# A new order of phase 1 in a linear-attention and SwiGLU block

## The chip, the cores and the metric

One core of a Trainium2 chip runs the whole kernel. The metric is the device time of one execution in microseconds (us), as a median over runs. One execution was also profiled, and its rows are what the argument below uses.

## The reference

A block on x of 2048 rows and 512 columns in bf16: a layer norm, a linear attention of 32 heads of 16 columns, and a SwiGLU feed-forward with 1792 hidden columns, both added to x.

```python
xn = layernorm(x)                                  # no gain, eps 1e-5
q, k, v = split(xn @ wqkv)                         # 32 heads of 16
phi = lambda t: where(t > 0, t + 1, exp(t)) + 1e-6
kv  = einsum("bhsd,bhse->bhde", phi(k), v);  z = phi(k).sum(over s)
o   = (phi(q) @ kv) / (phi(q) . z + 1e-6)
out = x + o @ wo + (silu(xn @ w_gate) * (xn @ w_up)) @ w_down
```

## The kernel before

The rows are cut into 16 tiles of 128. In phase 1 each tile t is normalised, turned so that its columns lie on the partitions, and projected to q and k; phi is applied; and G = xn^T phi(k) is summed over all tiles in four PSUM banks (0 to 3). v is never formed: G times the v weights gives kv afterwards. Phase 2 loops over 56 steps j (four chunks of 512 rows by 14 slices of the hidden columns): gate and up matmuls (`gu`, L526), SiLU on ScalarE (L534), the product on VectorE (`hop`, L539), and between them the output tiles (`ogroup`, L656 and L660).

Every operation goes through `K.add`, which records it with the tiles that it reads and writes. Each engine then runs its own operations strictly in the order of recording, and waits on semaphores where an operation needs another engine's result. So the order of phase 1 is one string of steps, written out by hand, that is read from left to right. Each word is a letter and a tile number, and goes to one engine:

- `S` (VectorE: row statistics, L251 and L254), `R` (ScalarE: rstd, L262 and L264), `L` (VectorE, L320) or `P` (GpSimd: a small step L335 and the normalising L338): xn of a tile.
- `D` (SyncE queue, L401): a DMA transpose of xn into `xnT`, by which tiles 4 to 15 get ready for their projections and tiles 0 to 2 for phase 2.
- `K`, `Q` (TensorE, L423): the projection of a tile to k or q, four matmuls of 512 columns into one bank; `K0:2` is only its part of weight chunk 2. The banks 4 to 7 are used in turn, so a projection also waits until the phi sum of the fourth before it has read its bank.
- `x`, `m`, `s` (for k) and `y`, `n`, `u` (for q): phi as exp on ScalarE (L441 or L444), a minimum on GpSimd (L451), and the sum on VectorE (L462).
- `G` (TensorE, L472): a tile's four matmuls into G.
- `l`, `T` (SyncE queue): loads of a tile of x, and of the large weights: T0 and T4 the halves of the gate weights, T1 and T5 those of the up weights, T2 the v weights, T3 wo, T6 the down weights.
- `U` (TensorE, ScalarE, VectorE): a step j of phase 2 done early.
- `F` (TensorE, L241): matmuls on constants that keep the engine busy; seven of them also open the kernel.

Tiles 0 to 2 (CENTRED) start the kernel, ahead of their statistics. Their x is only centred; the scale is applied later in phi. Tiles 0 and 2 are turned on TensorE by matmuls with the identity (`c`, L376), to which `d` (L384) adds minus the mean, taken from `nmb`, one column that either `M` (ScalarE, a copy of the tile with a running sum, L367), `O` (GpSimd, L370) or `a` (VectorE, L370) has written. Tile 1 has its mean from `M1` (ScalarE, L277), is centred by `C1` (VectorE, L292) and turned by `W1` (TensorE, L350). `e` and `h` (ScalarE, L393) take the two halves of tiles 0 and 2 out of PSUM into `xcT`, and `w`, `v`, `Y`, `Z` do it for whole tiles; tile 3 goes by `X3` and `Y3`. `j` (VectorE) and `J` (GpSimd, L312 and L315) make the centred and scaled tiles that G needs.

The first loads go out from two queues: four tiles of x and the eight 128 KB chunks of the q and k weights (`Q0` to `Q3`, `K0` to `K3`), six on SyncE's and six on ScalarE's.

Of the kernel before, what the change touches and what calls it, by code (L numbers as in the profile page):

```python
# [111 lines left out]
def bass_parallel_sum__linear_attn_block__swiglu_ffn__prompt_kernel(nc, A_x, A_wqkv, A_wo, B_x, B_w_gate, B_w_up, B_w_down, out):  # L112
# [5 lines left out]
    with contextlib.ExitStack() as es:  # L118
# [67 lines left out]
        def xload(eng, t):  # L186
            load(eng, ("x", t), x_sb[:, t, :], xin[t * P:(t + 1) * P, :])
# [22 lines left out]
        def wchunk(eng, i, c):  # L210
            load(eng, ("wqk", i, c), wqkv[:, c, i * D:(i + 1) * D], A_wqkv[c * P:(c + 1) * P, i * D:(i + 1) * D])

        for eng, text in (("sp", "x0 x1 Q0 Q3 K3 K0"),
                          ("act", "x2 Q1 x3 Q2 K2 K1")):
            for w in text.split():
                if w[0] == "x":
                    xload(eng, int(w[1:]))
                else:
                    wchunk(eng, int(w[0] == "K"), int(w[1:]))
# [336 lines left out]
        def run(text):  # L556
            words = [(w[0], int(w[1:].split(":")[0]), [int(c) for c in w.split(":")[1]] if ":" in w else None)
                     for w in text.split()]
            late = {t for k, t, _ in words if k == "z"}
            later.update({t: i for i, t in enumerate(t for k, t, _ in words if k == "u" and t in late)})  # L560
            for k, t, cs in words:
                steps[k](t) if cs is None else steps[k](t, cs)

        run("""
            M1 l4 c2 S0 c0 O0 S2 d0 a2 e0 d2 Q0:1 l13 e2 h0 Q0:0 C1 S1 l5 h2 W1 l7 Q2:01 Q0:3 S3 Q0:2 l11 R0
            Q2:3 Q2:2 r0 K0:2 l14 R3 j2 j0 K0:3 y0 J1 w1 L3 n0 K2:23 S4 y2 K0:01 l9 K2:1 K2:0 x0 x2 n2 X3 Y3
            K1:3 S13 m0 u0 Q1:123 m2 K1:12 K1:0 l6 R13 P13 s0 x1 s2 u2 T1 R4 Q1:0 l8 m1 K3 S9 y1 s1 l10 R9 x3 S5
            Q3 P4 D13 L9 D4 n1 G0 m3 y3 G2 G1 n3 u1 s3 P1 K13 Q13 x13 m13 K4 u3 G3 y13 S7 R5 s13 S14 D9 P5 K9 Q4
            S10 x4 m4 s4 n13 x9 u13 T2 G13 G4 D5 R10 K5 l12 R7 m9 P10 l15 y4 R14 Q9 P14 s9 Q5 S8 S6 x5 n4 D10 G9
            m5 u4 Q10 y9 R6 S15 y5 P7 s5 G5 R8 L6 y10 n9 u9 S12 K10 P0 n5 x10 n10 D14 u5 m10 D7 L8 D6 u10 D8 s10  # L570
            K14 Q14 K7 x14 T0 R15 D0 m14 y14 s14 Q6 S11 n14 x7 y6 u14 G14 R12 R11 m7 K8 P11 n6 s7 K6 Q7 L15 x6
            G7 x8 m6 D15 u6 s6 m8 Q8 D11 L2 P12 y8 n8 s8 y7 G6 K15 x15 n7 K11 m15 D12 x11 G10 u8 u7 m11 K12 T3
            Q11 s15 G8 y11 s11 x12 Q15 y15 Q12 m12 s12 D1 n11 D2 u11 n15 G11 G12 u15 y12 n12 T6 u12 T5 U0 U1 G15
            T4
        """)

        def gt_evac(c, eng):
# [181 lines left out]
```

## Time and profile before

| what | value |
|---|---|
| median of 3 runs | 212.54 us (212.4 to 212.63) |
| profiled execution, its own time | 212.36 us |
| its span in the profile | 211.1 us |
| TensorE busy | 206.5 us, 98% |
| VectorE, ScalarE, GpSimd busy | 122.3, 66.2, 67.4 us |

The execution's own time is 1.26 us more than its span, which runs from the first instruction to the last. In the rows below PE is TensorE's matmuls, PEld its weight loads, DVE VectorE, ACT ScalarE, POOL GpSimd, and SPq the issue of a DMA by SyncE. A row of the timeline is: start in us, duration in us, engine, line, operation, out<-in, shapes, count, and in brackets the idle time before it and what ended that. A row of the waits is: who waited for whom, us in total, times, the longest. A row of the DMA view is: tensors, queue and kind, count, KB of each, and the median us from issue to landing.

### The profile page before, as it was taken

How to read it: one execution, taken by the hardware profiler on the slowest of the kernel's cores; microseconds unless marked ns; L12 is line 12 of the kernel's file. 1: busy time of each engine (PE TensorE's matmuls, PEld its weight loads, DVE VectorE, ACT ScalarE, POOL GpSimd, SP SyncE). 2: the span in 40 equal slices, each digit the busy share in tenths (PEclk: the TensorE clock that was granted, in tenths of full speed). 3: DMA queues.
4: the chain of work that ended last, by engine and by line, in shares of the span. 5: the costliest groups of instructions: out<-in, count | busy, mean ns of one | idle time of the engine just before them, and what ended most of it. 6: DMA issues, size and time to landing. Idle time of an engine off the chain costs nothing.

```text
span 211.1 us, 2710 instructions
## 1 busy us (share of the span) xinstructions
PE 206.5 (98%) x992; PEld 96.2 (46%) x1011; DVE 122.3 (58%) x223; ACT 66.2 (31%) x135; POOL 67.4 (32%) x94
## 2 busy tenths in 40 slices
PE   7999999999999999999999999999999999999996
PEld 3444344444544444444444444444444444444455
DVE  3999986654885368454644773464457463625122
ACT  3985656454354333031221322130123031220000
POOL 3597776749950162202202021202202210000000
PEclk9999999999999999999999999999999999999999
DMA  6965739399501201110101110111001111011101
GB/s 183 361 203 151 126 66 233 64 285 366 184 0 25 53 0 27 22 50 28 25 25 42 32 30 25 25 48 26 28 26 24 25 50 51 3 50 26 49 28 50
DMA packets 28733, 16.43 MB, mean 78 GB/s; under 512 B 18608, under 2 KB 28592, under 8 KB 28720
## 3 DMA queue, kind: packets, MB, share of 16 engines
q1 hardware_dynamic: 27856, 15.48, 27.3%
q10 hardware_dynamic: 864, 0.79, 1.2%
q8 instruction: 8, 0.13, 0.3%
q14 instruction: 5, 0.04, 0.1%
HBM read 9.96 MB, written 2.10 MB: 57 GB/s over the span
## 4 chain that ended last, share of the span: by engine, by line
PE 93%; DMA 3%; ACT 1%; issue 1%; POOL 0%; SPq 0%; DVE 0%; POOLq 0%
PE pb L526 46%; PE pb L660 23%; PE pb L423 12%; PE pb L656 7%; PE pb L472 5%; DMA x_sb<-in_A_x_dram 2%; DMA xnT<-xn 2%; PE pb L584 0%; PE pb L650 0%; POOL xn L338 0%; ACT hT L277 0%; ACT ef L444 0%; PE pb L350 0%; SPq L184 0%; DVE out_sb L666 0%
## 5 line engine op out<-in xcount | busy, mean ns | idle before, releaser
L534 ACT ACTIVATE sil<-pb 128x512 bf16<-128x512 f32 x56 | 33.5, 597 | 102.9 <-PE pb L526 101.4
L539 DVE TENSOR_TENSOR hT<-pb,sil 128x512 bf16<-128x512 f32 x56 | 38.2, 683 | 38.9 <-PE pb L526 37.5
L526 PE MATMUL pb<-xnT,wg 128*128 128x512 bf16 x224 | 57.8, 379 | 0.0
L526 PE MATMUL pb<-xnT,wu 128*128 128x512 bf16 x215 | 57.3, 379 | 0.5
L617 POOL TENSOR_TENSOR pz<-pq,zbc 128x512 f32<-128x512 bf16 x16 | 22.3, 1397 | 91.0 <-DVE den L624 79.3
L660 PE MATMUL pb<-wd,hT 128*128 128x512 bf16 (+2 forms) x247 | 51.1, 355 | 0.3
L660 PEld LDWEIGHTS pb<-wd,hT 128*128 128x128 bf16 x252 | 23.6, 98 | 24.9
L526 PEld LDWEIGHTS pb<-xnT,wu 128*128 128x128 bf16 x224 | 21.9, 98 | 26.0
L526 PEld LDWEIGHTS pb<-xnT,wg 128*128 128x128 bf16 x224 | 21.9, 98 | 25.8
L666 DVE TENSOR_TENSOR out_sb<-pb,x_sb 128x512 bf16<-128x512 f32 (+2 forms) x18 | 11.4, 632 | 35.8 <-PE pb L660 35.8
L423 PE MATMUL pb<-wqkv,xnT 128*128 128x512 bf16 x103 | 24.0, 379 | 0.4 <-DMA xnT<-xn 0.4
L444 ACT ACTIVATE ef<-pb 128x512 bf16<-128x512 f32 x26 | 15.0, 593 | 13.7 <-PE pb L423 13.7
L451 POOL TENSOR_SCALAR ef<-ef 128x512 bf16<-128x512 bf16 x26 | 15.8, 616 | 6.5 <-ACT ef L444 6.5
L656 PE MATMUL pb<-M,pk 128*128 128x512 bf16 (+2 forms) x71 | 16.6, 355 | 0.1
L423 PEld LDWEIGHTS pb<-wqkv,xnT 128*128 128x128 bf16 x104 | 10.0, 98 | 13.1 <-DMA xnT<-xn 0.9
L472 PE MATMUL pb<-pk,xn 128*128 128x512 bf16 x50 | 12.9, 379 | 0.1
L251 DVE BATCH_NORM_STATS2 stats<-x_sb 128x6 f32<-128x512 bf16 x16 | 10.8, 677 | 3.3 <-DMA x_sb<-in_A_x_dram 3.3
L639 DVE TENSOR_TENSOR pq<-pq,rden 128x512 bf16<-128x512 bf16 x16 | 12.6, 786 | 0.0
L462 DVE SCALAR_TENSOR_TENSOR pk<-pb,ef 128x512 bf16<-128x512 f32 x13 | 8.8, 679 | 3.5 <-POOL ef L451 3.5
L462 DVE SCALAR_TENSOR_TENSOR pq<-pb,ef 128x512 bf16<-128x512 f32 x13 | 8.8, 684 | 3.6 <-POOL ef L451 3.5
L624 DVE TENSOR_REDUCE den<-pz 128x32 f32<-128x512 f32 x16 | 10.8, 676 | 0.0
L495 POOL TENSOR_TENSOR zacc<-zacc,pk 128x512 f32<-128x512 f32 x8 | 10.6, 1319 | 0.6
(71 smaller groups left out, 105.4 us busy)
## 6 DMA issues: line engine op xcount, KB each, us to landing
out_dram<-out_sb SPq DMA_DIRECT2D x15, 128.0 KB, 1.7
x_sb<-in_A_x_dram SPq DMA_DIRECT2D x14, 128.0 KB, 4.2
wu<-in_B_w_up_dram SPq DMA_DIRECT2D x2, 896.0 KB, 9.4
wg<-in_B_w_gate_dram SPq DMA_DIRECT2D x2, 896.0 KB, 9.3
wd<-in_B_w_down_dram SPq DMA_DIRECT2D x1, 1792.0 KB, 9.0
wqkv<-in_A_wqkv_dram ACTq DMA_DIRECT2D x4, 128.0 KB, 4.5
wqkv<-in_A_wqkv_dram SPq DMA_DIRECT2D x4, 128.0 KB, 4.2
wqkv<-in_A_wqkv_dram SPq DMA_DIRECT2D x1, 512.0 KB, 4.1
```

The costliest lines, as they stand in the source:

```text
L423: fns.append(lambda e, c=c, first=first, last=last: e.matmul(banks[b][:, :], src[:, c, t * P:(t + 1) * P], wqkv[:, c, col:col + D], start= ...
L444: K.add("act", lambda e: e.activation(buf, banks[b][:, :], ACT.Exp), r=[B(b)], w=[bkey])
L451: K.add("pool", lambda e: e.tensor_scalar(out=buf, in0=buf, scalar1=top, scalar2=0.0, op0=ALU.min, op1=ALU.max), r=[bkey] + tkeys, w=[bkey])
L462: K.add("dve", lambda e: e.scalar_tensor_tensor(out=dst, in0=val, scalar=low, in1=mid, op0=ALU.max, op1=ALU.add), r=keys + lkeys, w=[dkey])
L472: K.add("pe", [(lambda e, c=c: e.matmul(banks[c][:, :], src[:, t, c * P:(c + 1) * P], pk[:, t, :], start=first, stop=last)) for c in range ...
L526: fns.append(lambda e, c=c, b=b, w_=w_: e.matmul(banks[b][:, :], w_[:, c, fc * P:(fc + 1) * P], xnT[:, c, C * 512:(C + 1) * 512], start=(c ...
L534: K.add("act", lambda e: e.activation(sil[:, j % 2, :], banks[gb(j)][:, :], ACT.Silu), r=[B(gb(j))], w=[("sil", j % 2)])
L539: K.add("dve", lambda e: e.tensor_tensor(out=hT[:, C % 2, fc, :], in0=banks[gb(j) + 1][:, :], in1=sil[:, j % 2, :], op=ALU.mult), r=[B(gb( ...
L617: K.add("pool", lambda e: e.tensor_tensor(out=pz[:, t % 2, :].rearrange("q (g p) -> q g p", g=NG), in0=pq[:, t, :].rearrange("q (g p) -> q ...
L639: K.add("dve", lambda e: e.tensor_tensor(out=heads(pq[:, t, :]), in0=heads(pq[:, t, :]), in1=rden[:, i, :][:, :, None].broadcast_to([P, NH ...
L656: fns = [(lambda e, g=g: e.matmul(banks[bank][:, 0:hi - lo], pk[:, t, g * P:(g + 1) * P], M[:, g, lo:hi], start=(g == 0), stop=False)) for ...
L660: fns = [(lambda e, fc=fc: e.matmul(banks[bank][:, 0:hi - lo], hT[:, C % 2, fc, jj * P:(jj + 1) * P], wd[:, fc, lo:hi], start=False, stop= ...
```

## The change

The string of phase 1 is written anew, and the chunks of the weights are dealt anew to the two queues. What is computed stays the same, but for one more constant matmul (`F1`, 256 columns). In the order in which the engines meet it:

- Loads: Q0 and Q1 change queues, and K0, K1 and K3 change places.
- Start: the mean of tile 2 comes from ScalarE (`M2`) instead of VectorE (`a2`). ScalarE runs M2, M1, e0, h0, e2, h2 instead of M1, e0, e2, h0, h2. TensorE starts with Q0:0, F1, Q0:1, Q2:01 instead of Q0:1, Q0:0, W1, Q2:01.
- `J0` (GpSimd) and `j1` (VectorE) take the place of `J1` and `j0`.
- TensorE then runs K13 Q13 K4 K9 G3 Q4 G13 G4 Q9 K5 G9 Q10 Q5 G5 K10 K14 Q14 K7 G10 Q7 K6 G14 Q8 K8 K15 K11 Q6 Q15 Q11 K12 G7 G6 Q12 G8 G12 U0 G11 G15 U1, instead of K13 Q13 K4 G3 K9 Q4 G13 G4 K5 Q9 and so on to U0 U1 G15.
- SyncE's queue runs D13 D4 D9 l15 l12 D5 D10 T2 D14 D7 D6 D8 T3 D15 D1 D11 D0 D12 T0 D2 T6 T4 T5, instead of D13 D4 D9 T2 D5 l12 l15 D10 D14 D7 D6 D8 T0 D0 D15 D11 D12 T3 D1 D2 T6 T5 T4.
- Tiles 7, 11 and 12 are normalised on VectorE and tiles 2 and 6 on GpSimd, where it was the other way round.

```diff
-        for eng, text in (("sp", "x0 x1 Q0 Q3 K3 K0"),
-                          ("act", "x2 Q1 x3 Q2 K2 K1")):
+        for eng, text in (("sp", "x0 x1 Q1 Q3 K1 K3"),
+                          ("act", "x2 Q0 x3 Q2 K2 K0")):
...
         run("""
-            M1 l4 c2 S0 c0 O0 S2 d0 a2 e0 d2 Q0:1 l13 e2 h0 Q0:0 C1 S1 l5 h2 W1 l7 Q2:01 Q0:3 S3 Q0:2 l11 R0
-            Q2:3 Q2:2 r0 K0:2 l14 R3 j2 j0 K0:3 y0 J1 w1 L3 n0 K2:23 S4 y2 K0:01 l9 K2:1 K2:0 x0 x2 n2 X3 Y3
-            K1:3 S13 m0 u0 Q1:123 m2 K1:12 K1:0 l6 R13 P13 s0 x1 s2 u2 T1 R4 Q1:0 l8 m1 K3 S9 y1 s1 l10 R9 x3 S5
-            Q3 P4 D13 L9 D4 n1 G0 m3 y3 G2 G1 n3 u1 s3 P1 K13 Q13 x13 m13 K4 u3 G3 y13 S7 R5 s13 S14 D9 P5 K9 Q4
-            S10 x4 m4 s4 n13 x9 u13 T2 G13 G4 D5 R10 K5 l12 R7 m9 P10 l15 y4 R14 Q9 P14 s9 Q5 S8 S6 x5 n4 D10 G9
-            m5 u4 Q10 y9 R6 S15 y5 P7 s5 G5 R8 L6 y10 n9 u9 S12 K10 P0 n5 x10 n10 D14 u5 m10 D7 L8 D6 u10 D8 s10
-            K14 Q14 K7 x14 T0 R15 D0 m14 y14 s14 Q6 S11 n14 x7 y6 u14 G14 R12 R11 m7 K8 P11 n6 s7 K6 Q7 L15 x6
-            G7 x8 m6 D15 u6 s6 m8 Q8 D11 L2 P12 y8 n8 s8 y7 G6 K15 x15 n7 K11 m15 D12 x11 G10 u8 u7 m11 K12 T3
-            Q11 s15 G8 y11 s11 x12 Q15 y15 Q12 m12 s12 D1 n11 D2 u11 n15 G11 G12 u15 y12 n12 T6 u12 T5 U0 U1 G15
-            T4
+            c2 c0 M2 S0 S2 O0 d0 M1 e0 S1 h0 d2 Q0:0 e2 h2 F1 C1 Q0:1 Q2:01 l4 W1 S3 R0 l13 Q0:3 r0 l6 R3 l10
+            Q0:2 Q2:2 j2 j1 K0:1 y0 l11 L3 K0:2 Q2:3 y2 J0 n0 K2:12 n2 l7 K0:3 K0:0 w1 S4 K2:0 K2:3 K1:013 X3 x0
+            l8 S13 u0 x2 m0 Y3 s0 R13 m2 K1:2 Q1 P13 K3:02 l9 u2 x1 m1 K3:13 s2 S9 R4 l5 Q3 T1 y1 s1 R9 l14 L9
+            D13 x3 P4 D4 n1 G0 S10 G2 m3 y3 D9 n3 G1 K13 u1 s3 u3 x13 l15 S5 P1 m13 s13 Q13 K4 y13 R10 K9 R5 n13
+            G3 Q4 S14 x4 x9 P5 S7 m4 s4 G13 R7 y4 P10 u13 m9 l12 R14 n4 D5 S8 G4 D10 T2 Q9 s9 P2 S6 K5 x5 u4 S15
+            P14 L7 m5 y9 D14 G9 n9 Q10 Q5 R6 s5 u9 y10 S12 D7 R8 G5 K10 y5 n10 u10 L8 P6 K14 n5 x10 m10 x14 D6
+            u5 Q14 y14 D8 R15 s10 K7 S11 G10 L15 R12 x7 m14 s14 Q7 n14 R11 T3 u14 D15 y7 K6 m7 G14 s7 D1 Q8 P0
+            L11 D11 n7 L12 x6 u7 K8 y8 x8 m6 n8 K15 m8 s6 D0 D12 x15 u8 K11 x11 s8 m15 Q6 m11 T0 y6 n6 s15 Q15
+            Q11 s11 y15 K12 y11 u6 x12 G7 m12 G6 n11 Q12 y12 G8 s12 D2 T6 n12 n15 G12 u12 U0 G11 G15 u15 u11
+            U1 T4 T5
         """)
```

## The prediction

> **What bounds the kernel now.** First the page: the span, the engines' busy time, the granted clock, and the chain that ended last.
>
> ```profile
> span 211.1 us, 2710 instructions
> PE 206.5 (98%) x992; PEld 96.2 (46%) x1011; DVE 122.3 (58%) x223; ACT 66.2 (31%) x135; POOL 67.4 (32%) x94
> PEclk9999999999999999999999999999999999999999
> PE 93%; DMA 3%; ACT 1%; issue 1%; POOL 0%; SPq 0%; DVE 0%; POOLq 0%
> ```
>
> TensorE is busy for 98% of the span, at the full clock. The change keeps its matmuls (it adds one small one), so it can only win where PE waits. Second, the waits of PE alone:
>
> ```profile
> PE pb L423 <- DMA xnT<-xn: 0.4, 1, 0.4
> PE pb L384 <- DVE nmb L370: 0.3, 1, 0.3
> PE pb L423 <- ACT hT L393: 0.3, 1, 0.3
> ```
>
> That is all, apart from the launch. The whole purse is about 1 us, and each wait has to be found in the timeline. A matmul there lasts longer than its place in the stream, so I take the spacing from a long run: twenty in a row give (4.48 - 0.38) / 19 = 0.216 us each, and a group of four is 0.863 us.
>
> ```profile
> 28.57 4.48 PE L423 MATMUL pb<-wqkv,xnT 128*128 128x512 bf16 x20
> 20.91 1.61 PEld L472 LDWEIGHTS pb<-pk,xn 128*128 128x128 bf16 x8
> 21.13 1.89 PE L472 MATMUL pb<-pk,xn 128*128 128x512 bf16 x7
> 23.39 2.76 PE L423 MATMUL pb<-wqkv,xnT 128*128 128x512 bf16 x12 [0.37 <-DMA xnT<-xn]
> ```
>
> Eight weight loads stand at 20.91 and only seven matmuls at 21.13, so one record is missing. The stream was free again at 21.13 + 8 x 0.216 = 22.86 us, and the next matmul, K5, starts at 23.39. The wait cost 0.53 us, not the 0.37 printed. Third, the chain in order of time says what K5 waited for:
>
> ```profile
> 17.88 0.60 ACT ef L444
> ...
> 19.07 0.76 POOL xn L338
> 19.86 3.48 DMA xnT<-xn
> ```
>
> The transpose of tile 5 (step D5) took 3.48 us. The three before it took 2.4, and the median of all fifteen is 2.5 (first two rows below). In the stretch from 20.8 to 21.9 us a packet of another queue runs among D5's packets: one packet of q8, 5.6% of 16 engines over 1.1 us, which is 0.99 us of one DMA engine.
>
> ```profile
> xnT<-xn SPq DMA_TRANSPOSE x15, 2.5
> xnT<-xn SPq DMA_TRANSPOSE x3, 2.4
> q8 instruction: 1, 0.02, 5.6%
> xnT<-xn SPq DMA_TRANSPOSE x1, 3.5
> ```
>
> That is 3.48 - 2.4 = 1.08 us of delay beside a fetch of 0.99 us: I read it as the share of D5 on that engine standing behind the fetch.
>
> **The change part by part.** *The start.* The first projection starts at 5.89 and waits for L393, which on ACT follows the mean of tile 1 (L277), which waits for x1 to land.
>
> ```profile
> 1.27 3.56 DMA x_sb<-in_A_x_dram
> 4.85 0.63 ACT L277 ACTIVATE hT<-x_sb 128x512 bf16<-128x512 bf16 x1 [2.76 <-DMA x_sb<-in_A_x_dram]
> 5.47 1.19 ACT L393 ACTIVATE hT<-pb 128x256 bf16<-128x256 f32 x4
> 5.89 0.60 PE L423 MATMUL pb<-wqkv,hT 128*128 128x512 bf16 x2 [0.29 <-ACT hT L393]
> ```
>
> The new M2 (0.63 on ACT, plus about 0.19 for its sum) runs in the 2.76 us in which ACT is idle before 4.85, so it costs nothing, and d2 no longer waits for DVE. But M1, e0 and x1 keep their places and slots. PE therefore reaches the same wait earlier and leaves it at the same 5.89: the 0.3 of L384 does not vanish, it merges into the wait for e0. Gain 0. x1, the weights and x2 have equal sizes, 128 KB, and stand in equal slots, so which chunk lands in a slot changes only together with the projection that reads it (Q0:0 and Q0:1 change places). F1 is one matmul of 256 columns, half of the 512 that take 0.216: an estimate of 0.11. It fills time in which Q2:01 would wait for e2, now third on ACT instead of second: e2 ends one L393 pitch, (1.19 - 0.38) / 3 = 0.27, later. F1 costs 0 to 0.11. Against it stands a small stall before K3, the first projection at 11.63:
>
> ```profile
> 9.75 1.45 PEld L423 LDWEIGHTS pb<-wqkv,hT 128*128 128x128 bf16 x8
> 9.80 1.89 PE L423 MATMUL pb<-wqkv,hT 128*128 128x512 bf16 x7
> 11.63 1.89 PE L423 MATMUL pb<-wqkv,xnT 128*128 128x512 bf16 x8
> ```
>
> Eight matmuls from 9.80 end at 11.53, so K3 is 0.10 late for its evacuated tile. Pushed back by F1 it meets that tile in time. Net 0, bounds -0.1 to +0.15.
>
> *The wait at K5.* Before K5 the new order has K13, Q13, K4, K9, G3, Q4, G13, G4, Q9. From the end of Q13 to K5 that is 7 groups, 7 x 0.863 = 6.04 us (before: 6). D5 needs xn5 from POOL: Q13's last matmul drains about 0.2, then y13 0.60 (the L444 row above), n13 0.62, then P5's two steps, whose pitch is 0.30 + 0.76:
>
> ```profile
> 15.95 2.75 PE L423 MATMUL pb<-wqkv,xnT 128*128 128x512 bf16 x12
> 16.37 0.19 POOL L335 TENSOR_SCALAR nm<-mv 128x1 f32<-128x1 f32 x1
> 16.67 0.76 POOL L338 TENSOR_SCALAR xn<-x_sb,nm,rstd 128x512 bf16<-128x512 bf16 x1
> L451 POOL TENSOR_SCALAR ef<-ef 128x512 bf16<-128x512 bf16 x26 | 15.8, 616 | 6.5 <-ACT ef L444 6.5
> ```
>
> Together about 2.5 us after Q13. With a free 2.4 the transpose lands at 4.9 and K5 has 1.1 us to spare. With the whole 3.48 it lands at 5.98 against 6.04, and K5 just makes it or loses 0.1 (its weight load must come first). PE reaches the same count of instructions at about the same time, so the fetch stays where it is, while D5 is issued some 0.3 later (Q13, the second group of the run at 15.95, ended at 15.95 + 8 x 0.216 = 17.7, which makes 20.2 instead of 19.86), so less of the delay remains. I take 0 left of the 0.53; upper bound 0.1.
>
> *The rest of the transposes.* The early x loads change order within a run of equal 128 KB slots, and T1, not needed before U0, goes out one slot later. x15 and x12 leave SP ahead of D5, and T2 (512 KB) now stands behind D10. T3 (wo) comes before D15, D1, D11, D0 and D12, T0 (gate half) after them; T6, T4 and T5 still follow D2. The tightest is D11: xn15 waits for the phi sum of K10 and for S11. From K10's end: 0.2 + x10 0.60 + m10 0.62 + s10 0.68 + S11 0.68 and 0.18 + L15 0.40 = 3.36; D15 and D1 take SP 2.50; D11 needs the median 2.5: 8.36 us. PE has 10 groups between K10 and K11, 8.63 us. Margin 0.3, less 0.1 for the weight load: 0.2.
>
> ```profile
> L462 DVE SCALAR_TENSOR_TENSOR pk<-pb,ef 128x512 bf16<-128x512 f32 x13 | 8.8, 679 | 3.5 <-POOL ef L451 3.5
> L251 DVE BATCH_NORM_STATS2 stats<-x_sb 128x6 f32<-128x512 bf16 x16 | 10.8, 677 | 3.3 <-DMA x_sb<-in_A_x_dram 3.3
> 18.43 0.18 DVE L254 BATCH_NORM_AGGREGATE mv<-stats 128x2 f32<-128x6 f32 x1
> 37.62 0.40 DVE L320 TENSOR_SCALAR xn<-x_sb,mv,rstd 128x512 bf16<-128x512 bf16 x1
> 40.55 2.50 SPq L401 DMA_TRANSPOSE xnT<-xn  x2
> ```
>
> T0 goes out three SP slots after D11 (3 x 1.25 = 3.7) and D2 follows it by 0.6. D0, right behind T0, took 5.6 (first row below; the second is that of the two behind wo), so D2 lands 9.9 after D11's issue; U0 comes 10 groups after K11, at 2.5 + 0.3 + 8.6 = 11.4. It has 1.5 us.
>
> ```profile
> xnT<-xn SPq DMA_TRANSPOSE x1, 5.6
> xnT<-xn SPq DMA_TRANSPOSE x2, 3.9
> 47.57 1.03 PE L526 MATMUL pb<-xnT,wg 128*128 128x512 bf16 x4
> 49.57 0.69 DVE L539 TENSOR_TENSOR hT<-pb,sil 128x512 bf16<-128x512 f32 x1 [1.51 <-PE pb L526]
> ```
>
> U1 needs the bank of Q15, freed by u15, which on DVE now follows the product of U0. That product starts 2.00 after U0 (49.57 - 47.57) and u15 ends 0.6 + 0.69 later, at 3.3; U1 comes after U0, G11 and G15, at 4 x 0.863 = 3.45. Margin 0.15, less the weight load. DVE loses an operation on one column and gains one normalising of 0.40, POOL loses one, ACT gains M2: all of it lies under PE, as DVE is busy for 58% of the span.
>
> *Sum.* 212.36 (the profiled execution: span 211.1 and 1.26 around it) - 0.53 + 0 + 0 = 211.83 us. The median of the runs shown, 212.54, stands 0.18 above that execution, so I forecast 212.0 as a median, 0.25% faster. A measurement of this kernel can tell about 0.2% from no change, 0.42 us: the forecast lies only just beyond it.
>
> **A rule against it.** The Trainium skill, "Runtime: NRT & Kernel Launch", section "Instruction fetch mechanics", says that each engine is refilled in blocks of 256 instructions ahead of use, and that the cost of crossing a block is mostly hidden. By it the fetch would not be what made K5 wait, and the first rival below is left; the rows above (0.99 of fetch, 1.08 of delay) speak for the fetch.
>
> **The rivals.** *The load did it.* T2 went out on SP 2.66 us ahead of D5.
>
> ```profile
> 17.20 0.58 SPq L184 DMA_DIRECT2D wqkv<-in_A_wqkv_dram  x1
> wqkv<-in_A_wqkv_dram SPq DMA_DIRECT2D x1, 512.0 KB, 4.1
> ```
>
> If T2 delayed D5, the delay moves with it to D14, now the next transpose behind it. D5 landed 23.34 - 17.20 = 6.1 us after T2's issue; T2 now leaves one slot, 1.25, after D10, so D14 would land 7.4 after D10's issue. D10 leaves about 4.2 after Q13's end (D5's 2.5, then m4 0.62 and P10 1.06), and K14 comes 13 groups, 11.2, after it: 7.0. K14 waits 0.4 instead of K5's 0.53: 212.23, as a median 212.4. Against it: T2 had landed by 17.20 + 4.1 = 21.3, when a free D5 would still have had 1.0 us to go.
>
> *Small new waits.* K11, U1 and K3 have margins of 0.1 to 0.2 us, and my sums are no better than that. Each could lose 0.1 to 0.2: 0.1 to 0.4 in all, medians of 212.1 to 212.4.
>
> *Slower: wo ahead of D11.* The two transposes behind wo took 3.9 in the median (row above) against 2.5. If D11, third behind it, takes that too, K11 is late by 3.9 - 2.5 - 0.2 = 1.2, and 212.36 - 0.53 + 1.2 = 213.03, as a median 213.2. It turns the result beyond 0.2% once D11 takes more than 2.5 + 0.2 + 0.53 + 0.42 = 3.65. For it: 0.2 us of margin. Against it: D11 is issued at least 3.1 us after wo (its own 0.58 and two slots), and a load of that size lands in about 4.1.
>
> **How the numbers follow.** Forecast 0.58, the load 0.07, small new waits 0.20, wo ahead of D11 0.15. The forecast case is faster, and so is the first 0.02 of the small waits: 0.60. The rest of them and the load fall within 0.2%: 0.25. Slower 0.15. The range starts at 211.7 (the start's bound of -0.1, and 0.2 of spread between executions) and ends at 212.9, where the case of wo begins to turn the sign: left out are the worse part of that case and about 0.05 below.
>
> **What would show it.** In the profile after: no wait of PE on DMA xnT; the first projection still at about 5.9 us behind L393, with L384 no longer waiting; a D5 of 2.4 to 3.5 us with K5 right behind Q9; U0 near 46.2 us (47.57, less G11, less 0.53, give or take 0.1). A wait of PE on a DMA transpose at K14 speaks for the load, one at K11 for wo, and one on DVE L462 at U1 for the small waits. I am wrong if PE's waits after 6 us come to more than 0.1.

## The result and the profile after

The changed kernel takes 211.97 us (median of 9 runs, 211.54 to 212.37), the kernel before 212.54 in the runs beside it (9 runs, 212.34 to 213.18). The ratio is 0.9969, with a 95% interval of 0.9956 to 0.9981: faster by 0.3%. The profiled execution of the changed kernel took 211.76 us, against 212.36.

First the page of the changed kernel (span, busy time, the chain that ended last), then all that PE itself waited for:

```profile
span 210.5 us, 2725 instructions
PE 207.9 (99%) x1012; PEld 96.7 (46%) x1012; DVE 124.4 (59%) x223; ACT 67.2 (32%) x137; POOL 66.0 (31%) x92
...
PE 99%; DVE 0%; issue 0%
...
PE pb L241 <- PEq L744: 0.8, 1, 0.8
```

The chain, which was 93% PE with 3% DMA, is now PE from end to end, and the only wait left is the launch. (F1 is the one new matmul. The page counts 20 more because 19 matmul records are missing in the profile of the kernel before, which has 992 beside 1011 weight loads; the changed kernel's has 1012 of each.) The timeline of PE around the two places where time could change:

```profile
5.57 0.61 PE L423 MATMUL pb<-wqkv,hT 128*128 128x512 bf16 x1
5.97 0.35 PE L241 MATMUL pb<-const-bfloat16-1.0 128*128 128x256 bf16 x1
6.16 0.81 PE L423 MATMUL pb<-wqkv,hT 128*128 128x512 bf16 x3
...
11.57 1.89 PE L423 MATMUL pb<-wqkv,xnT 128*128 128x512 bf16 x8
...
21.07 1.89 PE L472 MATMUL pb<-pk,xn 128*128 128x512 bf16 x8
22.79 1.89 PE L423 MATMUL pb<-wqkv,xnT 128*128 128x512 bf16 x8
24.52 1.03 PE L472 MATMUL pb<-pk,xn 128*128 128x512 bf16 x4
...
46.10 1.03 PE L526 MATMUL pb<-xnT,wg 128*128 128x512 bf16 x4
```

K3 (11.57) starts 0.06 earlier than before (11.63). The eight matmuls from 21.07 end at 21.07 + 8 x 0.216 = 22.80 and Q9 and K5 follow without a gap: the 0.53 us is gone. 0.53 + 0.06 is the whole difference of the spans, 0.6.

The DMA view around the first stretch shows what became of D5 and of the fetch on queue q8. The fetch is the one large packet: 16 KB, in the slice marked 328 (slices of 0.05 us from 19.0, so at 19.6), after the last packets of x12.

```profile
GB/s 369 369 389 328 246 226 164 103 41 0 0 0 328 0 0 0 0 0 0 0 0 164 0 0 0 0 0 0 0 0 0 0 0 0 0 0 0 0 0 0
...
q8 instruction: 1, 0.02, 4.1%
...
xnT<-xn SPq DMA_TRANSPOSE x1, 2.4
```

It ran from 19.63 to 20.95 and was over before D5's packets began at 21.40; D5 was issued at 20.22 and landed at 22.65, in 2.4 us instead of 3.5. The rate of the DMA over the same three microseconds, 20.2 to 23.2 in slices of 0.075 us, first of the kernel before, then of the changed one:

```profile
GB/s 410 369 341 273 219 150 82 82 246 0 0 55 160 218 191 222 184 232 181 130 55 11 7 10 7 10 10 10 119 7 10 17 11 0 0 123 232 232 232 273
```

```profile
GB/s 0 0 0 0 0 0 0 0 0 0 0 0 0 0 0 3 92 198 232 225 212 218 218 198 109 39 4 0 0 0 0 0 0 0 0 0 0 72 188 225
```

This is what a held-up transpose looks like. Both show D5 as a hump of about 0.7 us near 200 GB/s. In the kernel before the hump has a tail: from 21.8 us, which is where the fetch (20.85 to 21.84) ends, the rate stands at 7 to 17 GB/s for 0.8 us (the 119 in it is one 8 KB packet of another queue, q14). The records of the single packets say what the tail is: D5 moves in 512 packets of 256 bytes, and exactly 32 of them, one sixteenth, begin after the fetch's end, one behind the other until 22.65. I read that as one DMA engine out of 16 doing its share alone, after the fetch. The transpose lands, at 23.34, only when that share is done. The hump itself is not late: D5's packets begin 1.2 us after its issue in both kernels (21.05 and 21.40), with T2 ahead of it or not.

### The profile page after: what moved, and what is told of

It reads as the page before. It is cut to its first block, busy times and chain, and to the rows that moved or that the text cites. A ratio compares the mean times of both kernels' runs of the same rounds, so it can differ in the third digit from the quotient of the medians.

```text
span 210.5 us, 2725 instructions
## 1 busy us (share of the span) xinstructions
PE 207.9 (99%) x1012; PEld 96.7 (46%) x1012; DVE 124.4 (59%) x223; ACT 67.2 (32%) x137; POOL 66.0 (31%) x92
## 4 chain that ended last, share of the span: by engine, by line
PE 99%; DVE 0%; issue 0%
PE pb L526 46%; PE pb L660 23%; PE pb L423 13%; PE pb L656 7%; PE pb L472 7%; PE pb L241 2%; PE pb L384 0%; PE pb L584 0%; PE pb L650 0%; PE pb L376 0%; PE pb L350 0%; DVE out_sb L666 0%
## 5 line engine op out<-in xcount | busy, mean ns | idle before, releaser
L251 DVE BATCH_NORM_STATS2 stats<-x_sb 128x6 f32<-128x512 bf16 x16 | 10.9, 678 | 3.5 <-DMA x_sb<-in_A_x_dram 3.4
```

## The experiments

Each was timed in five rounds beside the kernel before, whose median there was 212.54 to 212.66. "Span from K3" in the table is the span of the profiled execution less the start of K3, the first projection from `xnT`: it takes the start out, which varies between 11.24 and 11.99 us. The fetch is the start of the first 16 KB packet on q8, D5 its time from issue to landing.

| kernel | K3 | span from K3 | fetch | D5 | loss behind K3 | ratio and interval |
|---|---|---|---|---|---|---|
| before | 11.63 | 199.5 | 20.85 | 3.48 | K5 0.53 | |
| after | 11.57 | 198.9 | 19.63 | 2.44 | none | 0.9969 (0.9956 to 0.9981) |
| e1 | 11.39 | 199.0 | 18.80 | 2.42 | none | 0.9962 (0.9948 to 0.9977) |
| e2 | 11.72 | 199.5 | 20.93 | 3.46 | K5 0.51 | 0.9987 (0.9970 to 1.0003) |
| e3 | 11.50 | 199.6 | 19.14 | 2.42 | K13 0.62 | 0.9976 (0.9950 to 1.0002) |
| e4 | 11.61 | 199.0 | 19.37 | 2.42 | none | 0.9955 (0.9939 to 0.9971) |
| e5 | 11.53 | 199.0 | 20.78 | 3.36 | none | 0.9972 (0.9959 to 0.9986) |
| e6 | 11.70 | 199.5 | 19.84 | 2.44 | Q13 0.57 | 0.9990 (0.9977 to 1.0002) |
| e7 | 11.99 | 199.5 | 21.16 | 3.47 | K5 0.52 | 1.0003 (0.9988 to 1.0017) |
| e8 | 11.79 | 199.1 | 19.79 | 2.43 | 0.14 at 13.5 | 0.9974 (0.9962 to 0.9987) |
| e9 | 11.98 | 199.4 | 19.91 | 2.43 | last output 0.43 | 0.9994 (0.9983 to 1.0005) |
| e10 | 11.97 | 199.2 | 20.86 | 3.21 | K5 0.26 | 0.9997 (0.9982 to 1.0013) |
| e11 | 11.42 | 199.0 | 19.28 | 3.26 | none | 0.9976 (0.9965 to 0.9986) |
| e12 | 11.24 | 199.4 | 19.70 | 2.58 | last output 0.43 | 0.9991 (0.9974 to 1.0008) |

198.95 plus the loss in its row gives each "span from K3" within 0.1, so nothing else behind K3 moved the span by more than that. All of a row but its ratio comes from one profiled execution.

Theory A is the prediction's: the fetch runs at its own time and holds up D5; K5's later place saves the 0.53. Theory B is the first rival: the load T2, going out ahead of D5, does it. What the first runs led to is theory C: T2 holds the fetch back until it runs into D5, so both are needed, and either moving T2 or moving K5 is a cure.

**e1: only T2 is moved**, in the kernel before.

```diff
-S10 x4 m4 s4 n13 x9 u13 T2 G13 G4 D5 R10 K5 l12 R7 m9 P10 l15 y4 R14 Q9 P14 s9 Q5 S8 S6 x5 n4 D10 G9
+S10 x4 m4 s4 n13 x9 u13 G13 G4 D5 R10 K5 l12 R7 m9 P10 l15 y4 R14 Q9 P14 s9 Q5 S8 S6 x5 n4 D10 T2 G9
```

> The kernel before with one step moved: T2 (the v weights, 512 KB) goes out behind D10 instead of ahead of D5, as in the changed kernel. Fetch theory (D5 stands behind TensorE's first instruction fetch on one DMA engine): D5 still takes 3.3 to 3.5 us, K5 still waits about 0.5, 212.5 us, ratio 1.000. Load theory (D5 stands behind T2): D5 takes 2.4 to 2.5, K5 does not wait, 212.0, ratio 0.9975.

It took 211.9 us. PE's waits, then the DMA view from 18.0 to 19.6 (slices of 0.04 us):

```profile
PE pb L241 <- PEq L744: 0.8, 1, 0.8
```

```profile
GB/s 0 0 0 0 0 0 0 0 0 0 0 0 0 0 0 0 0 0 0 410 0 0 0 0 0 0 0 0 0 0 0 0 0 0 0 0 0 0 0 0
...
q8 instruction: 1, 0.02, 3.8%
```

With no load about, the fetch is alone in the stretch, at 18.8, and is over before D5's packets. One step moved in one string brings a gain that the runs can't tell from the whole change's. T2 had a part in it, against theory A.

**e2: fourteen more instructions ahead of the fetch**, in the kernel before: the seven filling matmuls as fourteen of half the width.

```diff
-        keep_busy(NWARM, 512)
+        keep_busy(2 * NWARM, 256)
```

> The kernel before with the seven opening matmuls of 512 constant columns cut into fourteen of 256: the same columns, seven more pairs of instructions ahead of the work. Fetch theory: the first fetch of q8 comes 7 x 0.216 = 1.5 us earlier in the work, at about 19.3, and is over before D5's packets start at about 21.0; D5 takes 2.4 to 2.5, K5 does not wait, 212.0 us, ratio 0.9975. Load theory: D5 still takes 3.5, 212.5 us, ratio 1.000.

212.47 us. Only TensorE has more instructions here, and the later fetches of q8 came earlier, the third by 1.6 us (67.87 instead of 69.51), the others by 0.1 to 7.9: q8 brings TensorE's instructions. The first fetch did not move: 20.93, and T2 landed at 21.37. K5 waited as before:

```profile
PE pb L423 <- DMA xnT<-xn: 0.3, 1, 0.3
```

So, with T2 ahead of it, the count of instructions doesn't set the first fetch's place.

**e3: the changed kernel with 23 narrow filling matmuls**, to put the fetch on D9.

```diff
-        keep_busy(NWARM, 512)
+        keep_busy(23, 156)
```

> The changed kernel with the opening 3584 constant columns cut into 23 matmuls of 156: 16 more pairs. Fetch theory: the first fetch comes 16 x 0.216 = 3.5 us earlier, at about 16.2 to 17.5, among D9's packets; D9 takes 3.3 to 3.5 instead of 2.5 and lands at about 19.1, K9 (due at 18.5) waits 0.4 to 0.6, and the time goes back to 212.4 to 212.6, ratio to before 1.000. Load theory: nothing changes, D9 takes 2.5, 212.0, ratio 0.9975.

A miss: the fetch moved by half a microsecond, to 19.14, and D9 took 2.51. In the profiled execution D13 took 3.75 us with no fetch on record beside it, and K13 waited:

```profile
16.43 1.90 PE L423 MATMUL pb<-wqkv,xnT 128*128 128x512 bf16 x8 [0.46 <-DMA xnT<-xn]
```

The load that left SP last before it landed 1.3 us later there than in the changed kernel (15.77 instead of 14.45), and D13 landed 0.62 behind that load. The median, 211.97, is the changed kernel's, so that execution was not a usual one. Why the load was late stays open.

The added instructions did put a later fetch on a transpose where no load is about, in phase 2. The transpose issued at 91.89 took 3.18 us; its counterpart in the changed kernel, with no fetch beside it, took 2.42. The DMA view of e3 from 91.9 to 95.0 us (slices of 0.0775 us; the lone 211 is the fetch, 92.33 to 93.54) has the same hump and tail as D5's:

```profile
GB/s 0 0 0 0 0 211 0 0 0 0 0 0 0 0 0 66 198 208 221 221 225 221 165 56 26 0 13 20 10 10 10 20 0 0 0 1 1 0 0 0
...
q8 instruction: 1, 0.02, 2.4%
...
pk<-pq SPq DMA_TRANSPOSE x1, 3.2
```

All loads have landed by 60 us. Of the 238 transposes behind that in the fourteen traces, 18 have a 16 KB fetch running between 1.0 and 2.4 us after their issue, and took 2.54 to 4.19 us; the other 220 took 2.38 to 2.50. So a fetch lengthens a transpose by itself, with no load ahead.

**e4: K5 back ahead of Q9**, in the changed kernel.

```diff
-G3 Q4 S14 x4 x9 P5 S7 m4 s4 G13 R7 y4 P10 u13 m9 l12 R14 n4 D5 S8 G4 D10 T2 Q9 s9 P2 S6 K5 x5 u4 S15
+G3 Q4 S14 x4 x9 P5 S7 m4 s4 G13 R7 y4 P10 u13 m9 l12 R14 n4 D5 S8 G4 D10 T2 K5 s9 P2 S6 Q9 x5 u4 S15
```

> The changed kernel with K5 and Q9 changing places, so that K5 stands one group (0.86 us) earlier. If the gain comes from the place of K5 (the prediction's reading, with the fetch among D5's packets): D5 lands at 23.1 to 23.7, K5 is due at 22.8 and waits 0.3 to 0.9, 212.3 to 212.9. If it comes from the fetch, which in the changed kernel began at 19.63 and was over at 20.95, ahead of D5's packets: D5 lands at 22.7, K5 does not wait or waits below 0.1, 212.0.

211.95 us. D5 took 2.42 and K5 did not wait. With T2 out of the way, K5's later place isn't needed. The start of this run is the one that the prediction described, waits and all:

```profile
PE pb L423 <- ACT hT L393: 0.9, 1, 0.9
...
5.86 0.39 PE L423 MATMUL pb<-wqkv,hT 128*128 128x512 bf16 x1 [0.85 <-ACT hT L393]
```

**e5: T2 back ahead of D5**, in the changed kernel, K5 in its later place.

```diff
-G3 Q4 S14 x4 x9 P5 S7 m4 s4 G13 R7 y4 P10 u13 m9 l12 R14 n4 D5 S8 G4 D10 T2 Q9 s9 P2 S6 K5 x5 u4 S15
+G3 Q4 S14 x4 x9 P5 S7 m4 s4 G13 R7 y4 P10 u13 T2 m9 l12 R14 n4 D5 S8 G4 D10 Q9 s9 P2 S6 K5 x5 u4 S15
```

> The changed kernel with one step moved: T2 goes out ahead of x12 and D5 again instead of behind D10, so that it leaves SP near 17.6 us, 2.6 ahead of D5, as before the change; K5 keeps its later place behind Q9. The prediction's step (the fetch of q8 holds D5 up wherever T2 stands, and K5's later place absorbs it): D5 about 3.4 us, K5 waits 0 to 0.1, no loss against the changed kernel: 212.0. T2 holds the fetch back (what the earlier runs suggest): T2 lands near 21.7, the fetch of q8 begins near 21 instead of 19.6, among D5's packets; D5 takes about 3.4 and lands near 23.6; K5, which stands at 22.8 + 0.86, waits 0 to 0.1 as well. Both give 212.0, but they differ in the fetch: near 19.6 by the first, near 21 by the second. The load alone, without a fetch: D5 lands at most 1.0 after T2, near 22.3 to 22.7, in 2.4 us.

212.07 us. T2 landed at 21.29, the fetch began at 20.78 instead of 19.63, D5 took 3.36 and landed at 23.54. The DMA view from 20.1 to 21.5 (slices of 0.035 us; the 849 is the fetch), and PE:

```profile
GB/s 380 293 322 439 410 468 380 263 351 468 410 468 234 351 410 439 439 410 205 849 323 293 322 176 205 293 293 410 117 29 30 0 0 0 0 0 51 59 183 168
...
q8 instruction: 1, 0.02, 4.8%
...
xnT<-xn SPq DMA_TRANSPOSE x1, 3.4
```

```profile
21.03 1.89 PE L472 MATMUL pb<-pk,xn 128*128 128x512 bf16 x8
22.76 1.89 PE L423 MATMUL pb<-wqkv,xnT 128*128 128x512 bf16 x8
```

This tells A from C: the fetch goes where T2 puts it. The q14 packet that stood in D5's tail in the kernel before is at 21.05 here, ahead of D5's own, and D5 is as late; so it wasn't the cause. It also shows the prediction's own cure at work: Q9 takes 22.76 to 23.62, D5 lands at 23.54, and K5 starts at 23.62 with 0.08 us to spare.

**e6 and e11: the old start, the new rest.** The dealing of the chunks and the string up to `R9 x3` are those of before, what follows is the changed kernel's. In e6 the step S5 was left at its old, earlier place; e11 has it where the changed kernel has it. The diff is from e6 to e11.

```diff
-S5 Q3 L9 D13 P4 D4 n1 G0 S10 G2 m3 y3 D9 n3 G1 K13 u1 s3 u3 x13 l15 P1 m13 s13 Q13 K4 y13 R10 K9 R5
+Q3 L9 D13 P4 D4 n1 G0 S10 G2 m3 y3 D9 n3 G1 K13 u1 s3 u3 x13 l15 S5 P1 m13 s13 Q13 K4 y13 R10 K9 R5
```

> The kernel before with its own start (its first 60 or so steps and its dealing of the chunks) and the changed order from T1 on. If the gain is the one wait at K5: D5 2.4 us, no wait at K5, fetch of q8 near 19.6, the first projection as before; 211.9 to 212.0, ratio 0.997. If the new start carries a part of the gain (in the profile of the changed kernel K3 came 0.06 us earlier): 0.1 less gain, 212.1.

212.44 us for e6: the wait at K5 was gone, and one of 0.57 had come (16.02 + 4 x 0.216 = 16.88, then 17.45):

```profile
16.02 1.03 PE L423 MATMUL pb<-wqkv,xnT 128*128 128x512 bf16 x4
17.45 2.76 PE L423 MATMUL pb<-wqkv,xnT 128*128 128x512 bf16 x12 [0.41 <-DVE pq L462]
```

The 0.86 us of S5 on DVE (0.68 on L251 and 0.18 on L254) stood ahead of u1 and u3, whose banks the next projections take. So the total looked as if the new rest were worth nothing.

> The splice of the old start and the new rest once more, with one step mended: S5 (0.86 us of DVE) stood ahead of its place in the new order and made u1 late, so that K13's successor waited 0.41 for its bank. Here S5 stands behind l15, as in the changed kernel. If the gain is the one wait at K5: no wait on DVE L462 at 17 us, D5 2.4, no wait at K5; 212.0, ratio 0.997. If the new rest needs the new start: a wait at 17 us stays, 212.3 or more.

212.05 us for e11, no wait of PE but the launch. With S5 in its place the rest alone has the gain. In this run D5's row reads 3.26, though its packets ran undisturbed from 21.25 to 22.2 and the fetch was over at 20.45; K5, in its later place, did not feel it.

**e7: the new start, the old rest.** The changed kernel, with the old order behind T1; the two lines stand for all that follow.

```diff
-D13 x3 P4 D4 n1 G0 S10 G2 m3 y3 D9 n3 G1 K13 u1 s3 u3 x13 l15 S5 P1 m13 s13 Q13 K4 y13 R10 K9 R5 n13
+S5 Q3 P4 D13 L9 D4 n1 G0 m3 y3 G2 G1 n3 u1 s3 P1 K13 Q13 x13 m13 K4 u3 G3 y13 S7 R5 s13 S14 D9 P5
```

> The changed start and the changed dealing of the chunks, with the old order from T1 on, T2 ahead of D5 and K5 ahead of Q9. If the start is worth nothing: the fetch near 20.9, D5 about 3.4, K5 waits 0.5; 212.4 to 212.6, ratio 0.998 to 1.000. If the start is worth something by itself: below 212.2.

212.86 us, ratio 1.0003 (0.9988 to 1.0017): no gain that the runs can tell. K5 waited again, 21.49 + 8 x 0.216 = 23.22 to 23.74:

```profile
21.49 1.89 PE L472 MATMUL pb<-pk,xn 128*128 128x512 bf16 x8
23.74 2.55 PE L423 MATMUL pb<-wqkv,xnT 128*128 128x512 bf16 x11 [0.36 <-DMA xnT<-xn]
```

**e8: M1 behind e0, h0 and e2**, an attempt at a faster version.

```diff
-c2 c0 M2 S0 S2 O0 d0 M1 e0 S1 h0 d2 Q0:0 e2 h2 F1 C1 Q0:1 Q2:01 l4 W1 S3 R0 l13 Q0:3 r0 l6 R3 l10
+c2 c0 M2 S0 S2 O0 d0 e0 h0 S1 d2 e2 M1 Q0:0 h2 F1 Q0:1 Q2:01 l4 C1 S3 R0 l13 Q0:3 r0 l6 R3 l10 Q0:2
```

> The changed kernel with the start dealt once more: M1, which waits for x1, goes behind the evacuations e0, h0 and e2 on ACT, so that the first projection no longer waits for x1's landing; nothing else moves but the places of h0, W1 and C1 in the first 12 us. If the first projection is held by x1 through M1 and e0: it starts near 5.3 instead of 5.6 to 5.9, and the sum gains 0.1 to 0.2 where x1 lands late, 211.8; but the chunk that the second projection needs lands at 5.7, so part of it turns into a wait for DMA wqkv. If PE's early clock or the chunks hold the start anyway: 212.0, no difference.

212.27 us. The first projection started at 5.43, and then PE waited for the next chunk; K3 came at 11.79, no earlier. In this run, with x1 out of the way, a weight chunk holds the start.

```profile
5.43 0.39 PE L423 MATMUL pb<-wqkv,hT 128*128 128x512 bf16 x1
5.66 0.27 PE L241 MATMUL pb<-const-bfloat16-1.0 128*128 128x256 bf16 x1
6.31 1.53 PE L423 MATMUL pb<-wqkv,hT 128*128 128x512 bf16 x6 [0.38 <-DMA wqkv<-in_A_wqkv_dram]
```

**e9: T2 cut in halves**, in the kernel before: 256 KB ahead of D5, 256 KB behind D10. The first use of the v weights waits for both.

```diff
-               lambda: wload("sp", 2), lambda: woload("sp"),
+               lambda: wload("sp", 2, 0, 2), lambda: woload("sp"),
...
-               lambda: dload("sp")]
+               lambda: dload("sp"), lambda: wload("sp", 2, 1, 2)]
...
-n4 D10 G9
+n4 D10 T7 G9
...
```

> The kernel before; T2 is cut in two halves of 256 KB: the first stays where T2 was, 2.66 us ahead of D5, the second goes out behind D10. K5 keeps its place. If a load ahead of D5 costs whatever its end: D5 3.4, K5 waits 0.5; 212.5, ratio 0.999. If the load matters by its end, because it holds the fetch of q8 back until then: the half lands near 19.3 to 19.6, the fetch begins near 19, as where no load stands ahead (18.8), and is over at 20 to 20.4; D5 2.4 to 2.5, no wait at K5; 211.9 to 212.0, ratio 0.996 to 0.997.

D5 went as theory C said: the half landed at 20.36, the fetch ran from 19.91 to 20.91, D5 took 2.43, and K5, in its old place, did not wait. The DMA view from 19.5 to 20.5 (slices of 0.025 us; the 656 is the fetch):

```profile
GB/s 451 451 328 451 246 492 451 287 328 246 328 205 246 123 123 41 656 0 0 0 0 0 0 0 0 0 0 0 0 0 0 0 0 0 0 0 0 0 0 0
...
q8 instruction: 1, 0.02, 6.2%
...
xnT<-xn SPq DMA_TRANSPOSE x1, 2.4
```

The time missed: 212.49. K3 began 0.35 late, and the last write of the output took 1.87 us from issue to landing instead of 1.44. A fetch on q14 at 210.17, 0.71 us behind the write's issue, lies in it; in the changed kernel that fetch comes at 210.65, 1.6 us behind the issue, when the last write has landed. The DMA views of the last write, changed kernel and e9:

```profile
out_dram<-out_sb SPq DMA_DIRECT2D x1, 32.0 KB, 1.4
```

```profile
q14 instruction: 1, 0.01, 1.0%
...
out_dram<-out_sb SPq DMA_DIRECT2D x1, 32.0 KB, 1.9
```

**e12: the same cut in the changed kernel**, to tell the start from the cut.

```diff
-G3 Q4 S14 x4 x9 P5 S7 m4 s4 G13 R7 y4 P10 u13 m9 l12 R14 n4 D5 S8 G4 D10 T2 Q9 s9 P2 S6 K5 x5 u4 S15
+G3 Q4 S14 x4 x9 P5 S7 m4 s4 G13 R7 y4 P10 u13 T2 m9 l12 R14 n4 D5 S8 G4 D10 T7 Q9 s9 P2 S6 K5 x5 u4 S15
```

> The changed kernel with T2 cut in halves: 256 KB ahead of x12 and D5, where the run with the whole T2 there had a fetch of q8 at 20.8 and a D5 of 3.36, and 256 KB behind D10. In the kernel before, the half T2 let D5 go in 2.43, but that run's time did not show the gain: its weight chunks landed 0.3 to 0.8 later in the first 9 us, and K3 began 0.35 later. If the chunks' landing is chance or belongs to one build, and the cut costs nothing: fetch before 20.3, D5 2.4 to 2.5, no wait of PE behind 12 us; 211.9 to 212.1, ratio 0.996 to 0.998. If cutting T2 itself costs about 0.5 us (the second part's wait at the first M, or a later end of the outputs): no wait at K5, and still 212.4 to 212.5, ratio 0.999, whatever the start.

212.44 us: the cut costs. In the profiled execution (211.88 us, the lowest of the twelve) K3 was the earliest of all, 11.24, D5 took 2.58, nothing waited at K5, PE's last matmuls began 0.33 us before the changed kernel's, and yet the span was 210.6: the last write took 1.87 us again, with the q14 fetch at 209.43 in it, again 0.71 behind the issue. In both kernels with the one DMA instruction more, that fetch came forward into the last write.

**e10: the kernel before with 23 narrow filling matmuls.**

```diff
-        keep_busy(NWARM, 512)
+        keep_busy(23, 156)
```

> The kernel before with the seven filling matmuls of 512 columns at the start as 23 of 156 columns: the same PE time, 32 instructions more ahead of the fetch, which the later fetches showed as 3.4 us earlier (two thirds of that with 14 more). T2 and K5 keep their places. If T2 by itself delays D5: D5 3.4, K5 waits 0.5; 212.5. If the fetch does, and can run before T2 leaves at 17.2: D5 2.4 (it lands 1.0 behind T2), no wait at K5, 212.0; D13, D4 or D9 may take the delay instead, and K13, K4 or K9 wait up to 0.6, which would bring it back to 212.5. If the fetch waits for T2's end whatever its count: at 20.9 as before, D5 3.4, 212.5.

212.7 us. The third fetch came 3.7 us earlier (65.78), the first stayed at 20.86, again in T2's last microsecond (T2 landed at 21.60); D5 took 3.21 and K5 waited 0.26. It is the third of the outcomes named, with half the wait expected at K5: with T2 ahead, the fetch stays near T2's end whatever its count.

## Why the prediction was right, point by point

*The sum held.* 211.83 us was forecast for the profiled execution and 211.76 measured; 212.0 for the median, and 211.97 measured. It is one wait of 0.53 us, and the runs that keep it (e2) or bring it back (e7) show no gain clear of the noise. That the profiled execution agrees within 0.1 is partly luck: the nine runs spread from 211.54 to 212.37.

*The start: net 0, as far as the runs can tell.* e7, the new start alone, has a ratio of 1.0003, and its interval is about 0.3 us to either side: the forecast's bounds of -0.1 and +0.15 are too narrow to be tested. The merged wait for e0 at 5.86 stands in e4 as forecast. The forecast of 5.9 for the first projection did not hold in the changed kernel's own profile: it starts at 5.57 with no wait there, because x1 landed at 4.19 instead of 4.82 (in e4, with the same start, x1 landed at 4.79). x1 landed between 4.0 and 4.8 in these runs, and the last weight chunk between 8.07 and 9.02, not in step with x1. K3 moved by 0.75 us over kernels whose starts are partly identical (e9's is the kernel before's, at 11.98 against 11.63). Over the profiled executions that is more than any loss in the table; what moves the landings was not shown.

*The mechanism at K5: right in the fetch and in the cure, wrong in one premise.* That one engine's share of D5 stood behind the 0.99 us fetch is what the tail in the DMA rates shows, and the transpose of phase 2 in e3 shows it with no load about. That K5's later place is enough is what e5 shows, with 0.08 us to spare where the prediction had 0.06. The step that failed is "the fetch stays where it is". It moved from 20.85 to 19.63, because T2 no longer stood before it, and that brought D5 down to a free 2.44; its later issue (20.2 forecast, 20.22 measured) was not needed for it. The change has two cures, and either is enough: e1 and e4 have T2's alone, e5 has K5's alone. That T2's move was one of them was not foreseen, and the total can't show it.

*The rival "the load did it" was half right.* I set it against the fetch, and the runs join them: with the whole of T2 ahead, in five kernels, the fetch began between 20.78 and 21.16; with half of it 19.70 and 19.91; with only tiles of x, 19.14 to 19.84; with no load, 18.80. In all but the last it began 0.1 to 0.8 us before that load, or the last of those tiles, landed. A load by itself does lengthen a transpose close behind it, as the rival said: D14, now issued 2.0 us behind T2 and with no 16 KB fetch beside it, took 3.46. But it landed 0.58 behind T2, and D5 in the kernel before 2.04 behind it, with a sixteenth of its packets behind the fetch. K14, which was to wait 0.4, did not wait.

*The other rivals did not come.* D11 took 2.50 us behind wo, U0 started at 46.10 (46.2 forecast), and U1's thin margin shows only as a wait of 0.2 of its weight load, not of PE.

*The rule against it.* The Trainium skill, "Runtime: NRT & Kernel Launch", section "Instruction fetch mechanics", has the cost of crossing a block mostly hidden. The traces agree for seven of the eight 16 KB fetches of a run, beside which PE waits for nothing. The one that met a transpose with a waiting projection cost 0.53 us of PE, by the row of K5. "Mostly" is where the exception lies.

No run here beats the changed kernel by more than the runs can tell: e1 (0.9962), e4 (0.9955) and e11 (0.9976) lie within its interval or overlap it.

## What to carry to other kernels

Two things made a transfer here a microsecond longer than its equals: a load ahead of it that had not landed (D14), and a single packet on one of its DMA engines (D5). The second shows in the rate by time as a tail near a sixteenth of the peak; look at what ends where the tail begins. Ask what put that packet there before moving the consumer, because moving the earlier load can be a second cure: here it took one step (e1). And when parts are tested alone, compare spans from a fixed landmark behind the start: here a start that varied by 0.75 us, a misplaced 0.86 us step (e6) and a last write 0.43 longer (e9, e12) each hid a gain of 0.53 that was there.

## What was not expected of the hardware

- An instruction fetch did not come by the count of instructions alone. 32 instructions more moved the third fetch by 3.7 us and the first by nothing (e10); a 512 KB load moved the first by 2.0 (18.80 to 20.85). What makes it yield to loads was not shown.
- The last output write took 1.87 us instead of 1.44, twice, with a q14 fetch beside its packets, though the packets themselves were through in 0.30 us instead of 0.26. e11's D5 (3.26 us, packets over at 22.2, a q14 fetch at 21.81 to 22.16) may be of the same kind. No run took that fetch away by itself, so it stays a coincidence seen three times.
- D13's 3.75 us in e3 stands beside a load that landed 1.3 us late just ahead of it; why that load was late is not on record.
